# Attention with 512 heads on one core: other forms of loading K and V (4 KB rows, strided V, one head in eight transposed by DMA), and V fetched at K's lead

## Chip, cores, metric

The kernel runs on one core of a Trainium2 chip. The metric is the device time of one execution in microseconds (us); quoted times are medians of several executions. All executions told of here were fast (granted TensorE clock 0.96 to 1.00). One core has a matrix engine (TensorE, "PE" in the profile, its weight loads "PEld"), a vector engine (VectorE, "DVE"), an activation engine (ScalarE, "ACT"), GpSimd ("POOL"), and SyncE ("SP"), which in this kernel does nothing but issue DMAs.

## The reference

```python
B, H, Sq, Sk, D = 16, 32, 192, 1024, 128          # bf16
def reference(q, k, v):
    scale = q.shape[-1] ** -0.5
    scores = jnp.einsum("bhqd,bhkd->bhqk", q, k) * scale
    return jnp.einsum("bhqk,bhkd->bhqd", softmax(scores, axis=-1), v)
```

There are 512 heads, worked on as 256 pairs. Each head has 256 KB of K, 256 KB of V, 48 KB of Q and 48 KB of output.

## The kernel before

The products need K with D on the partitions, so TensorE transposes each head's K: a batch of 16 transposes goes into one PSUM bank (`f_k`) and VectorE copies it to `f_kt`. Then come the scores (`f_s`), the exponential on ScalarE (`f_pt`), P·V into a single output bank (`f_o`), and the normalisation on VectorE. GpSimd copies V from its landing ring (`f_vs`) to `f_vp`. Q is transposed by the DMA itself. K and Q have rings of four pairs, V a ring of ten.

```python
def load_k(p):                                     # 512 KB, rows of 2 KB
    if p >= R: e.wait_ge(s_tr, 2 * (p - R) + 2)    # R = 4: the ring's old K is transposed
    e.dma_start(kn[:, p % R, :]..., kf[2*p:2*p+2].rearrange("x (m t) d -> m x (t d)", t=T))
def load_q(p):                                     # 96 KB, transposed by the DMA
    if p >= R: e.wait_ge(s_qk, 2 * (p - R) + 2)    # the scores of the ring's old pair are done
    e.dma_start_transpose(qt[:, p % R], qf[2*p:2*p+2]...)
def load_v(p):                                     # 512 KB, ring of NVS = 10 pairs
    if p >= NVS: e.wait_ge(s_pv, p - NVS + 1)
    e.dma_start(vs[:, p % NVS], vf[2*p:2*p+2]...)
# ... SyncE's order in the steady part:
for n in range(NPR + 2):
    load_k(n + R); load_q(n + R)
    load_v(n - 2 + NVS)
    if (n - 2) % GP == 0: store((n - 2) // GP - 1) # GP = 4 pairs a store
# ... TensorE's order:
def step(n):
    for x in range(2):                             # x: the two heads of a pair
        qk(2 * n + x)                              # waits for Q, and for the old exponential
        tr(n + 1 + x, 1 - x)                       # one batch of K transposes; waits for K
        pv(n - 2, 12 * x, 12 * x + 12)             # half of P·V of the pair before last;
                                                   # the first half waits for the output bank
# ... VectorE, once a pair:
def onorm(p):
    dve.wait_ge(s_pv, p + 1)
    dve.reciprocal(ri, O[:, :, 128]); dve.tensor_tensor(ob..., O..., ri..., ALU.mult)  # then s_on
```

Of the kernel before, what the change touches and what calls it, by code (L numbers as in the profile page):

```python
# [395 lines left out]
HINT = False  # L396
# [6 lines left out]
def _attention_kernel(nc, q, k, v, out, NVS=10):  # L403
# [3 lines left out]
    NH = B * H  # L407
# [14 lines left out]

    with ExitStack() as outer:
# [6 lines left out]
        s_kn = [sem("f_kn%d" % i) for i in range(R)]  # L430
        s_q = [sem("f_q%d" % i) for i in range(R)]
        s_v = [sem("f_v%d" % i) for i in range(NVS)]
# [13 lines left out]
        with ExitStack() as es:  # L446
# [7 lines left out]
            kn = sb("f_kn", [128, R, 2 * T * D], BF16)  # L454
# [3 lines left out]

            vs = sb("f_vs", [128, NVS, 2, T * D], BF16)
# [11 lines left out]

            block = es.enter_context(nc.Block())

            @block.sync
            def _(e):
                def load_k(p):
                    if p >= R:
                        e.wait_ge(s_tr, 2 * (p - R) + 2)
                    e.dma_start(
                        kn[:, p % R, :].rearrange("m (x c) -> m x c", x=2),  # L480
                        kf[2 * p:2 * p + 2].rearrange("x (m t) d -> m x (t d)", t=T),
                    ).then_inc(s_kn[p % R], 16)

                def load_q(p):
                    if p >= R:
                        e.wait_ge(s_qk, 2 * (p - R) + 2)
                    e.dma_start_transpose(
                        qt[:, p % R, :, :],
                        qf[2 * p:2 * p + 2].rearrange("g (p j) d -> (g p) (j d)", j=3),
                    ).then_inc(s_q[p % R], 16)  # L490

                def load_v(p):
                    if p >= NVS:
                        e.wait_ge(s_pv, p - NVS + 1)
                    e.dma_start(
                        vs[:, p % NVS, :, :],
                        vf[2 * p:2 * p + 2].rearrange("x (m t) d -> m x (t d)", t=T),
                    ).then_inc(s_v[p % NVS], 16)

                def store(g):  # L500
                    so = g % NSO
                    h0 = 2 * GP * g
                    last = GP * (g + 1) == NPR
                    if last:
                        e.wait_ge(s_fin, 1)
                    else:
                        e.wait_ge(s_rc, GP * (g + 1) + 1)
                    e.dma_start(
                        of[h0:h0 + 2 * GP].rearrange("(a x) (p j) d -> (x p) a (j d)", x=2, j=3),
                        ob[:, so, :, :],  # L510
                    ).then_inc(s_st[so], 16)

                load_k(0)
                load_q(0)
                load_k(1)
                load_q(1)
                load_v(0)
                for p in range(2, R):
                    load_k(p)
                    load_q(p)  # L520
                    load_v(p - 1)
                for p in range(R - 1, min(NVS, NPR)):
                    load_v(p)
                for n in range(NPR + 2):
                    if n + R < NPR:
                        load_k(n + R)
                        load_q(n + R)
                    if n >= 2 and n - 2 + NVS < NPR:
                        load_v(n - 2 + NVS)
                    if n >= 3 and (n - 2) % GP == 0:  # L530
                        store((n - 2) // GP - 1)
                store(NPR // GP - 1)
                for so in range(min(NSO, NPR // GP)):
                    e.wait_ge(s_st[so], 16 * len(range(so, NPR // GP, NSO)))

            @block.gpsimd
            def _(gp):
                gp.memset(ones[:], 1.0).then_inc(s_set, 1)  # L538
                gp.wait_ge(s_set, 1)
                gp.affine_select(  # L540
                    ident[:], ones[:], [[1, 128]], ALU.is_equal, 0.0, base=0, channel_multiplier=-1
                ).then_inc(s_set, 1)
                gp.memset(vp[:, :, :, D:VB], 1.0).then_inc(s_set, 1)  # L543
                for p in range(NPR):
                    gp.wait_ge(s_v[p % NVS], 16 * (p // NVS + 1))
                    if p >= R:
                        gp.wait_ge(s_pv, p - R + 1)
                    gp.tensor_copy(  # L548
                        vp[:, p % R, :, 0:D].bitcast(U32),
                        vs[:, p % NVS, :, :].rearrange("p x (t d) -> p (x t) d", d=D).bitcast(U32),  # L550
                    ).then_inc(s_vp, 1)

            @block.tensor
            def _(pe):
# [4 lines left out]
                def tr(p, y):  # L559
                    if y == 0:  # L560
                        take(s_kn[p % R], 16)
                    if (p, y) != (0, 0):
                        take(s_ev, 1)
                    ins = None
                    for t in range(T):
                        for z in range(2):
                            c0 = (8 * y + t) * D + 64 * z
                            ins = pe.transpose(  # L568
                                k_ps[64 * z: 64 * z + 64, t * 128: t * 128 + 128],
                                kn[:, p % R, c0: c0 + 64], ident[:], tile_position=(0, 64 * z))  # L570
                    ins.then_inc(s_tr, 1)

                def qk(h):
                    p, x = divmod(h, 2)
                    if x == 0:
                        take(s_q[p % R], 16)
                        if p == NPR - 1:
                            take(s_ev, 1)
                    if h >= 2:
                        take(s_exp, 1)  # L580
                    S = s_ps[x]
                    ins = None
                    for t in range(T):
                        cut = {2: (0, 2, 3), 5: (0, 1, 3)}.get(t, (0, 3))
                        for j0, j1 in zip(cut[:-1], cut[1:]):
                            mv = qt[:, p % R, j0:j1, 64 * x: 64 * x + 64]
                            c0 = t * SQ + j0 * 64
                            for w in range(2):
                                ins = pe.matmul(  # L589
                                    S[64 * w: 64 * w + 64, c0: c0 + (j1 - j0) * 64],  # L590
                                    kt[:, p % R, 8 * x + t, 64 * w: 64 * w + 64], mv,
                                    start=True, stop=True, tile_position=(0, 64 * w))
# [4 lines left out]
                def pv(p, lo, hi):  # L597
                    if lo == 0:
                        take(s_vp, 1)
                        if p >= NPR - 1:  # L600
                            take(s_exp, 2)
                        if p >= 1:
                            take(s_on, 1)
                    ins = None
                    for j, t in order[lo:hi]:
                        for x in range(2):
                            ins = pe.matmul(  # L607
                                o_ps[64 * x: 64 * x + 64, j * 129: j * 129 + 129],
# [7 lines left out]
                def step(n):  # L616
                    for x in range(2):
                        if n < NPR:
                            qk(2 * n + x)
                        if n + 1 + x < NPR:  # L620
                            tr(n + 1 + x, 1 - x)
                        if n >= 2:
                            pv(n - 2, 12 * x, 12 * x + 12)

                pe.wait_ge(s_set, 3)
                tr(0, 0)
                tr(0, 1)
                tr(1, 0)
# [3 lines left out]
                with nc.Fori(0, loops, engines=[mybir.EngineType.PE], hint_back_edge=HINT,  # L632
# [10 lines left out]
            def _(dve):  # L643
                cnt = [0]

                def done(ins):
                    ins.then_inc(s_dv, 1)
                    cnt[0] += 1
                    dve.wait_ge(s_dv, cnt[0])

                def evac(p, y):
                    dve.wait_ge(s_tr, 2 * p + y + 1)
                    if p >= R:
                        dve.wait_ge(s_qk, 2 * (p - R) + 2)
                    dve.tensor_copy(  # L655
# [3 lines left out]

                def onorm(p):  # L660
                    g, a = divmod(p, GP)
                    so = g % NSO
                    O = o_ps[:, 0:387].rearrange("p (j c) -> p j c", j=3)
# [4 lines left out]
                    if a == 0 and g >= NSO:  # L668
                        dve.wait_ge(s_st[so], 16 * (g // NSO))
# [7 lines left out]
                def check(lo, hi, i):  # L677
                    done(dve.tensor_scalar(chk[:, lo:hi], rinv[:, lo:hi], 1.0 / RS_HI, 1.0 / RS_LO, ALU.max, ALU.min))  # L678
                    done(dve.tensor_tensor(chk[:, lo:hi], chk[:, lo:hi], rinv[:, lo:hi], ALU.not_equal))  # L679
                    done(dve.tensor_reduce(bad[:, i: i + 1], chk[:, lo:hi], mybir.AxisListType.X, ALU.max))  # L680

                early = max(NPR - 6, 1)
                evac(0, 0)
                evac(0, 1)
                evac(1, 0)
                for n in range(NPR + 2):
                    for x in range(2):
                        if n + 1 + x < NPR:
                            evac(n + 1 + x, 1 - x)
                    if n >= 2:  # L690
                        onorm(n - 2)
                        if n - 2 == early - 1:
                            check(0, 3 * early, 0)
                check(3 * early, 3 * NPR, 1)
# [52 lines left out]
```

## Time and profile before

| before | |
|---|---|
| time | 984.85 us (981.81 to 985.28, four runs) |
| period of eight heads in the steady part | 14.67 us |
| first exponential; exponential of head 32; last exponential | 10.9; 86.9; 967.1 us |
| SyncE in one period: issuing / waiting on semaphores | 10.0 / 4.6 us |

The period is the mean distance between exponentials eight heads apart, over heads 48 to 464 of the trace.

The next lines are from the profile page of before: the span, the busy times, two groups of instructions (line, engine, operation, output<-inputs, count | busy us, mean ns of one | idle before it and what ended that), and the DMA issues (count, size, median us from issue to landing).

```profile
span 982.0 us, 67627 instructions
PE 948.1 (97%) x30722; PEld 945.6 (96%) x30722; DVE 546.1 (56%) x1031; ACT 743.6 (76%) x513; POOL 267.7 (27%) x263
...
L655 DVE COPY f_kt<-f_k 128x1024 bf16<-128x1024 bf16 x512 | 354.0, 691 | 408.6 <-PE f_k L568 408.6
...
L568 PE MATMUL f_k<-f_ident,f_kn 128*64 128x128 bf16 x8192 | 331.3, 220 | 18.5 <-PEq L557 18.5
...
f_kn<-in_k_dram SPq DMA_DIRECT2D x256, 512.0 KB, 5.9
f_vs<-in_v_dram SPq DMA_DIRECT2D x256, 512.0 KB, 5.1
...
f_qt<-in_q_dram SPq DMA_TRANSPOSE x256, 4.9
```

One stretch of 50 us from the windows view of before follows (busy us of each engine, granted clock, DMA share, GB/s).

```profile
core 0: us, PE busy (x) PEld busy (x) DVE busy (x) ACT busy (x) POOL busy (x), PEclk, DMA share, GB/s
...
450.00:500.00 50.00, 50.00 (x1645) 50.00 (x1642) 28.39 (x55) 39.65 (x28) 14.00 (x14) 1.00 1.08 349
```

TensorE is busy without a gap and limits the steady part. Of its 18.5 us of idle before K transposes, 16.6 lie in the first 60 us and 1.9 near the end, at 954. The DMA share of 1.08 says that the packets' times fill all 16 DMA engines as well. The timeline of TensorE in before (start, duration, line, what) shows one head:

```profile
516.95 0.86 PE L589 MATMUL f_s<-f_qt,f_kt 128*64 128x192 bf16 x20
517.62 0.64 PE L568 MATMUL f_k<-f_ident,f_kn 128*64 128x128 bf16 x16
518.07 0.89 PE L607 MATMUL f_o<-f_vp,f_pt 128*64 128x129 bf16 x24
518.77 0.86 PE L589 MATMUL f_s<-f_qt,f_kt 128*64 128x192 bf16 x20
```

From start to start, scores take 0.67 us, the batch 0.45 and half of P·V 0.70.

### The profile page before, as it was taken

The numbers are of one execution on the slowest core, as the hardware profiler recorded it, in microseconds if no ns is written. First come the engines' busy times: TensorE is split into PE (matmuls) and PEld (weight loads), VectorE is DVE, ScalarE is ACT, GpSimd is POOL, SyncE is SP. The second block draws the span as 40 slices with busy tenths as digits, with TensorE's granted clock in tenths as the row PEclk, the third lists the DMA queues.
The fourth block names the chain that finished last, engine by engine and source line by source line (L and its number), as shares of the span: only waits on it lengthen the run. The fifth ranks groups of instructions, "written<-read, shape, count | busy, mean of one in ns | idle before, by whom it ended". The sixth has DMA issues, their size and how long they took to land. (4 is left out here: it accounts for less than half of the span.)

```text
span 982.0 us, 67627 instructions
## 1 busy us (share of the span) xinstructions
PE 948.1 (97%) x30722; PEld 945.6 (96%) x30722; DVE 546.1 (56%) x1031; ACT 743.6 (76%) x513; POOL 267.7 (27%) x263
## 2 busy tenths in 40 slices
PE   5699999999999999999999999999999999999995
PEld 4699999999999999999999999999999999999995
DVE  2355555555556555555555555655555555565562
ACT  4377777777777777777777777777777777777773
POOL 2122222222222222222222222222222222222220
PEclk9799999999999999999999999999999999999998
DMA  9999999999999999999999999999999999999971
GB/s 296 256 259 349 351 347 325 354 329 353 329 348 343 332 342 341 346 328 342 351 326 344 334 350 320 361 340 301 367 349 335 350 316 347 358 336 335 347 235 38
DMA packets 279602, 319.35 MB, mean 325 GB/s; under 512 B 115712, under 2 KB 148480, under 8 KB 279552
## 3 DMA queue, kind: packets, MB, share of 16 engines
q1 hardware_dynamic: 279552, 318.84, 102.5%
q14 instruction: 37, 0.30, 0.1%
q8 instruction: 13, 0.21, 0.1%
HBM read 268.44 MB, written 25.17 MB: 299 GB/s over the span
## 5 line engine op out<-in xcount | busy, mean ns | idle before, releaser
L706 ACT ACTIVATE f_pt<-f_s 128x1536 bf16<-128x1536 f32 x512 | 742.4, 1450 | 224.1 <-PE f_s L589 223.9
L655 DVE COPY f_kt<-f_k 128x1024 bf16<-128x1024 bf16 x512 | 354.0, 691 | 408.6 <-PE f_k L568 408.6
L607 PE MATMUL f_o<-f_vp,f_pt 128*64 128x129 bf16 x12288 | 458.7, 221 | 2.2 <-PEq L557 2.2
L548 POOL COPY f_vp<-f_vs 128x1024 uint32<-128x1024 uint32 x256 | 266.8, 1042 | 694.0 <-PE f_o L607 678.9
L589 PE MATMUL f_s<-f_qt,f_kt 128*64 128x192 bf16 (+2 forms) x10240 | 443.5, 231 | 4.2 <-issue 4.2
L607 PEld LDWEIGHTS f_o<-f_vp,f_pt 128*64 128x64 bf16 x12288 | 394.9, 110 | 2.7 <-issue 2.7
L589 PEld LDWEIGHTS f_s<-f_qt,f_kt 128*64 128x64 bf16 x10240 | 359.8, 111 | 4.5 <-issue 4.5
L568 PE MATMUL f_k<-f_ident,f_kn 128*64 128x128 bf16 x8192 | 331.3, 220 | 18.5 <-PEq L557 18.5
L568 PEld LDWEIGHTS f_k<-f_ident,f_kn 128*64 128x64 bf16 x8192 | 288.3, 111 | 20.0 <-issue 19.8
L670 DVE TENSOR_TENSOR f_ob<-f_o,f_rinv 128x384 bf16<-128x384 f32 x256 | 142.7, 557 | 8.9
L666 DVE RECIPROCAL f_rinv<-f_o 128x3 f32<-128x3 f32 x256 | 46.2, 181 | 10.6 <-PE f_o L607 8.0
L706 ACT ACT_TABLE_LOAD x1 | 1.3, 1283 | 0.8 <-PEq L732 0.8
L639 PEld LDWEIGHTS f_o<-f_bad,f_ones 128*1 128x1 bf16 x1 | 0.1, 79 | 1.6 <-DVEq L695 1.6
L639 PE MATMUL f_o<-f_bad,f_ones 128*1 128x1 bf16 x1 | 0.2, 164 | 1.4 <-DVEq L695 1.4
L679 DVE TENSOR_TENSOR f_chk<-f_chk,f_rinv 128x750 f32<-128x750 f32 (+1 forms) x2 | 1.1, 560 | 0.1
L680 DVE TENSOR_REDUCE f_bad<-f_chk 128x1 bf16<-128x750 f32 (+1 forms) x2 | 1.1, 555 | 0.1
L678 DVE TENSOR_SCALAR f_chk<-f_rinv 128x750 f32<-128x750 f32 (+1 forms) x2 | 1.0, 508 | 0.0
L697 DVE CAST redo<-f_o 1x1 int32<-1x1 f32 x1 | 0.1, 147 | 0.3 <-PE f_o L640 0.3
L540 POOL TENSOR_SCALAR_AFFINE_SELECT f_ident<-f_ones 128x128 bf16<-128x128 bf16 x1 | 0.3, 292 | 0.1
L538 POOL MEMSET f_ones<- 128x128 bf16 x1 | 0.2, 204 | 0.3 <-POOLq L732 0.3
L543 POOL MEMSET f_vp<- 128x128 bf16 x1 | 0.2, 211 | 0.0
L732 POOL MEMSET const-float32-0.0<- 128x1 f32 x1 | 0.1, 98 | 0.3 <-issue 0.3
(5 smaller groups left out, 0.5 us busy)
## 6 DMA issues: line engine op xcount, KB each, us to landing
f_kn<-in_k_dram SPq DMA_DIRECT2D x256, 512.0 KB, 5.9
f_vs<-in_v_dram SPq DMA_DIRECT2D x256, 512.0 KB, 5.1
out_dram<-f_ob SPq DMA_DIRECT2D x64, 384.0 KB, 5.0
f_qt<-in_q_dram SPq DMA_TRANSPOSE x256, 4.9
```

The costliest lines, as they stand in the source:

```text
L548: gp.tensor_copy(vp[:, p % R, :, 0:D].bitcast(U32), vs[:, p % NVS, :, :].rearrange("p x (t d) -> p (x t) d", d=D).bitcast(U32),).then_inc( ...
L568: ins = pe.transpose(k_ps[64 * z: 64 * z + 64, t * 128: t * 128 + 128], kn[:, p % R, c0: c0 + 64], ident[:], tile_position=(0, 64 * z))
L589: ins = pe.matmul(S[64 * w: 64 * w + 64, c0: c0 + (j1 - j0) * 64], kt[:, p % R, 8 * x + t, 64 * w: 64 * w + 64], mv, start=True, stop=True ...
L607: ins = pe.matmul(o_ps[64 * x: 64 * x + 64, j * 129: j * 129 + 129], pt[:, (2 * p + x) % NP, t * SQ + j * 64: t * SQ + j * 64 + 64], vp[:, ...
L639: pe.matmul(o_ps[0:1, 0:1], ones[:, 0:1], bad[:, 0:1], start=True, stop=False)
L655: dve.tensor_copy(kt[:, p % R, 8 * y: 8 * y + 8, :], k_ps[:].rearrange("d (t c) -> d t c", c=128),).then_inc(s_ev, 1)
L666: dve.reciprocal(ri, O[:, :, 128]).then_inc(s_rc, 1)
L670: dve.tensor_tensor(ob[:, so, a, :].rearrange("p (j d) -> p j d", j=3), O[:, :, 0:128], ri.unsqueeze(2).to_broadcast([128, 3, D]), ALU.mul ...
L678: done(dve.tensor_scalar(chk[:, lo:hi], rinv[:, lo:hi], 1.0 / RS_HI, 1.0 / RS_LO, ALU.max, ALU.min))
L679: done(dve.tensor_tensor(chk[:, lo:hi], chk[:, lo:hi], rinv[:, lo:hi], ALU.not_equal))
L680: done(dve.tensor_reduce(bad[:, i: i + 1], chk[:, lo:hi], mybir.AxisListType.X, ALU.max))
L706: act.activation(pt[:, h % NP, :], s_ps[h % 2][:], ACT_FN.Exp, scale=scale).then_inc(s_exp, 1)
```

## The change

The intent is to relieve TensorE: in each unit of eight heads (four pairs) the last head's K is transposed by the DMA, straight into `f_kt`, so TensorE does 448 batches and not 512. Below, "Kx" is the DMA that transposes this K, and a "period" is the time of one unit. To pay for Kx on the DMA's side, the K of the first three pairs comes in rows of 4 KB (for this K fewer, larger packets). That puts the keys in another order, so V of these six heads must land at every fourth partition: four strided DMAs of 384 KB, issued as one block of 1.5 MB. V is fetched only one unit ahead, at the lead of K, in place of ten pairs ahead. In each unit the slot after head 4 has no batch. There are smaller edits at the ends: eight dummy matmuls at the start, output banks that alternate in the last two pairs, a last store of one pair, and a check on VectorE spread over three steps.

```diff
-def _attention_kernel(nc, q, k, v, out, NVS=10):
+def _attention_kernel(nc, q, k, v, out, NVU=2):
                 def load_k(p):
+                    if p % R == 3:
+                        plain_k(p, 0, s_kn[3])                       # head 6 of the unit, 2 KB rows
+                        if p >= R:
+                            e.wait_ge(s_qk, 2 * (p - R) + 2)
+                        e.dma_start_transpose(                       # head 7: "Kx" below
+                            kt[:, 3, T: 2 * T, :], kf[2 * p + 1].rearrange("(m t) d -> m (t d)", t=T),
+                        ).then_inc(s_kx, 16)
+                    # ...
+                        e.dma_start(kn[:, p % R, :, :],
+                            kf[2 * p:2 * p + 2].rearrange("x (m s) d -> (x m) (s d)", s=2 * T))   # 4 KB rows
+                def load_va(u):                                      # "V block" below
+                    for c in range(4):
+                        e.dma_start(
+                            vs[c:128:4, u % NVU, 0:6, :],
+                            vf[h:h + 6].rearrange(
+                                "x (m b a t) d -> a b m x (t d)", b=2, a=2, t=T)[c // 2, c % 2],
+                        ).then_inc(s_va[u % NVU], 16)
                 for n in range(NPR + 2):
                     if n + R < NPR:
                         load_k(n + R)
                         load_q(n + R)
-                    if n >= 2 and n - 2 + NVS < NPR:
-                        load_v(n - 2 + NVS)
+                    u = n // R + 1
+                    if u < NPR // R:
+                        if n % R == 0:
+                            load_va(u)
+                        if n % R == 1:
+                            load_vb(u)                               # V of the unit's last pair, plain
# ... transposes of the 4 KB rows write every second pair of bf16 in PSUM:
+                            kp = k_ps[:, 256 * t: 256 * t + 256].rearrange(
+                                "d (m a b) -> d m a b", a=2, b=2)[:, :, a, :]
# ... TensorE's step (VectorE's likewise):
-                        if n + 1 + x < NPR:
-                            tr(n + 1 + x, 1 - x)
+                        if h < NH and h % 8 != 4:
+                            tr(7 * (h // 8) + h % 8 + (3 if h % 8 < 4 else 2))
# ... (semaphores, buffers, start and end cut)
```

## The prediction

> **What bounds it now.** In the steady part TensorE does: in the windows table from 400 to 550 us it is busy 50.00 of every 50 us at clock 1.00. The timeline shows exponentials on ScalarE every 1.833 us, one per head, 1.45 us long, so ScalarE is not the limit. Per head TensorE spends about 0.67 us on scores, 0.46 on a K transpose batch, 0.70 on half of P·V. 512 heads are 939 us; the other 43 us of the 982 us span are the ends. Beginning: from its seventh head on ScalarE is 17.4 us further behind than at its first; TensorE idles 9.6 us from 19.8 and 4.2 us from 44.2, because K and Q of pairs 4 onward stand in the DMA queue behind ten pairs of V; afterwards it restarts at a low clock (0.79 and 0.88 in the windows to 60 us). End: a 1.9 us gap at 954 behind the check on VectorE, two 1.0 us gaps where P·V waits for the single output bank, 7 us of last store.
>
> DMA is close behind: 340 GB/s, share 1.05-1.08 in those windows. But Q and K land about 7 us before use (landing median 4.9 and 5.9 us), so it is not the limit yet.
>
> **What the change does.**
> 1. 64 of 512 transpose batches leave TensorE, with their VectorE copies: QK start to PV start is 1.11-1.16 us with a batch, 0.67 without. 64 x 0.46 = 29 us, all critical.
> 2. Beginning: only four pairs of V ahead, K of head 0 first, eight dummy matmuls for the clock: 11-14 of the 17 us back.
> 3. End: check spread, output banks alternate, last store is one pair: 3-5 us.
> 4. DMA work rises. Packets in the trace take 18 ns (256 B), 36 (768 B), 84 (2048 B), 9 (semaphore): about 9 ns fixed each. The Trainium skill (DMA: Bandwidth & Descriptors, "Why small descriptors are slow") states a fixed per-packet overhead; the trace agrees. My estimate for 4 KB is 158 ns. Per four pairs and engine: before 13.9 us of packets in a 14.67 us period; after, 4 KB rows save 0.2, the transposed head (1024 packets of 256 B for 128 of 2 KB) costs 0.5: 14.2 us. TensorE's new period is 14.67 - 0.46 = 14.21. DMA and TensorE become equal, and DMA takes back some: period 14.2-14.6.
>
> Strided PSUM writes: the skill (PSUM - Partial Sum Buffer, "Specifications") says non-contiguous patterns slow matmuls. Here pairs of bf16 stay together; no line of this trace shows such a write. I expect no slowing, and little from V's stride.
>
> **Sum.** 985 - 29 (transposes) - 12 (beginning) - 4 (end) + 8 (DMA) = 948 us. Range 932 to 968. Faster by over 2%: 0.85; within 2%: 0.09; slower: 0.06.
>
> **What would show it.** Right: 448 K copies on VectorE, transpose matmuls at about the old 220 ns; no TensorE gap over 3 us in the first 60 us; exponentials averaging 1.78-1.82 us apart; Q and K landing later than before. DMA as the limit would show as short TensorE waits for K or Q, repeating every four pairs.
>
> **What would make it wrong.** Transposes into strided PSUM slower (0.44 us per batch more would cost 170 us). The DMA transpose holding the queue: transfers nearly stop for 0.5-1.7 us around Q transposes in this trace; one more per four pairs could eat the gain. V at stride four colliding within DMA. Or DMA gaining more from 4 KB rows, giving under 940.

## More of the kernel before

SyncE in one period: issuing / waiting on semaphores 10.0 / 4.6 us. SyncE's times are sums over 40 periods of the trace's DMA issue records, with the 0.04 us between them counted as issuing.

SyncE's timeline in before shows the even order, one V behind each K and Q, with free time (501.83 to 503.17) in which it waits:

```profile
499.50 1.19 SPq L487 DMA_TRANSPOSE f_qt<-in_q_dram  x1
500.73 0.59 SPq L495 DMA_DIRECT2D f_vs<-in_v_dram  x1
501.36 0.47 SPq L479 DMA_DIRECT2D f_kn<-in_k_dram  x1
503.17 1.19 SPq L487 DMA_TRANSPOSE f_qt<-in_q_dram  x1
```

## The result, and the profile after

| | before | after |
|---|---|---|
| time, us | 984.85 | 1074.07 (1070.18 to 1075.53, four runs) |
| ratio to before | | 1.0907 (95%: 1.0869 to 1.0945) |
| period of eight heads, us | 14.67 | 16.17 |
| exponential of head 32, us | 86.9 | 82.7 |
| last exponential to the end, us | 14.95 | 15.1 |
| SyncE in one period: issuing / waiting, us | 10.0 / 4.6 | 15.8 / 0.5 |

A ratio here is the mean time of one kernel's fast runs over that of the other's of the same rounds, so it is not quite the ratio of the medians quoted. The change made the kernel 9% slower. The steady part explains it: from head 32 on, 60 periods times 1.50 us are 90 us more; the beginning gives about 4 us back.

The page of after:

```profile
span 1068.6 us, 65473 instructions
PE 942.6 (88%) x29706; PEld 913.8 (86%) x29706; DVE 502.0 (47%) x967; ACT 743.6 (70%) x513; POOL 267.3 (25%) x263
...
L750 DVE COPY f_kt<-f_k 128x1024 bf16<-128x1024 bf16 x448 | 309.9, 692 | 538.0 <-PE f_k L656 535.8
...
L656 PE MATMUL f_k<-f_ident,f_kn 128*64 128x128 bf16 x7168 | 286.9, 219 | 91.2 <-PEq L630 88.5
...
f_kn<-in_k_dram SPq DMA_DIRECT2D x189, 512.0 KB, 7.2
f_vs<-in_v_dram SPq DMA_DIRECT2D x252, 384.0 KB, 5.6
...
f_kt<-in_k_dram SPq DMA_TRANSPOSE x64, 7.1
```

The 64 batches are gone (448 copies), and a transpose takes as long as before, 219 ns against 220, although it now writes with a stride. (Matmul ends are modelled in this profile; the starts say the same: from a batch to the next P·V 0.45 us in both.) But TensorE has 12% of the span idle (3% before), of which 91 us stand before K transposes. A K of 512 KB lands 7.2 us after its issue, not 5.9, and Kx after 7.1; a strided part of V, at 5.6, is little later than the 5.1 of before, the plain V of the unit's last pair lands after 7.0. A stretch of the windows view of after says the same, 45.4 us busy of 50:

```profile
450.00:500.00 50.00, 45.44 (x1452) 44.30 (x1448) 24.62 (x49) 36.05 (x26) 12.49 (x12) 1.00 1.02 309
```

The waits view of after counts them (who waited for whom: us in total, times, longest):

```profile
PE f_k L656 <- PEq L630: 88.5, 69, 4.2
PEld f_o L699 <- issue: 30.3, 65, 0.5
PE f_o L699 <- PEq L630: 18.1, 63, 0.3
```

Both kinds come once per unit: 69 and 63 times for 64 units. In the distances of the exponentials, by place in the unit, seven of the eight are 1.82 to 1.86 us as before, the one across the slot without a batch included (1.85), and the one from a unit's head 7 to the next unit's head 0 is 3.30 in place of 1.82. So two things went wrong: the removed batch saved nothing, and a stall of 1.48 us came in.

The timeline of after shows both:

```profile
512.40 0.56 DVE L770 TENSOR_TENSOR f_ob<-f_o,f_rinv 128x384 bf16<-128x384 f32 x1
...
513.11 0.89 PE L699 MATMUL f_o<-f_vp,f_pt 128*64 128x129 bf16 x24 [0.29 <-PEq L630]
...
518.67 4.59 SPq L519 DMA_TRANSPOSE f_kt<-in_k_dram  x1
...
523.30 1.26 SPq L534 DMA_TRANSPOSE f_qt<-in_q_dram  x1
...
524.61 0.58 SPq L526 DMA_DIRECT2D f_kn<-in_k_dram  x1
...
525.23 1.18 SPq L534 DMA_TRANSPOSE f_qt<-in_q_dram  x1
...
526.46 2.59 SPq L551 DMA_DIRECT2D f_vs<-in_v_dram  x4
...
529.09 0.60 SPq L526 DMA_DIRECT2D f_kn<-in_k_dram  x1
...
534.04 0.86 PE L680 MATMUL f_s<-f_qt,f_kt 128*64 128x192 bf16 x20
...
536.84 0.64 PE L656 MATMUL f_k<-f_ident,f_kn 128*64 128x128 bf16 x16 [1.94 <-PEq L630]
```

*The slot without a batch (513).* It lies between scores of an even head and the first half of the next P·V, which needs the single output bank. The pair before has just been normalised, 512.40 to 512.96, and P·V starts at 513.11, after a wait. Before, the batch filled this time. The weight loads' 30.3 us of waits, 65 times, stand where the 29 us were to be saved; e1 below tests this.

*The stall (536.84).* SyncE starts Kx at 518.67, and the issue itself takes 4.59 us. Then come Q, K, Q, the V block, and only then, at 529.09, the K that TensorE wants next; the trace has it land at 536.55, 7.46 us later. TensorE finished the scores before it at 534.9 and waits 1.94 us. Between 517.82 and 529.69 SyncE has no gap of more than 0.05 us. Over the steady part it waits 0.5 of 16.2 us and is busy issuing for the rest. That is the row of the table that changed most, and the prediction has no term for it.

A warning on reading: the profile's list of SyncE's own waits puts 230.6 us, 63 times, to Kx waiting for scores. Releasers are inferred, and there the inference took an event that fell inside the long issue. The record's start is the better witness: in the median Kx starts 0.50 us after the issue before it, within 0.01 us of the exponential of the head whose scores it needs, and its issue then takes 3.9 us. So the wait is 0.5 us, and the rest is issue.

### The profile page after: what moved, and what is told of

Same layout as the page of the kernel before. It is cut to its first block, busy times and chain, and to the rows that moved or that the text cites. A ratio compares the mean times of both kernels' runs of the same rounds, so it can differ in the third digit from the quotient of the medians.

```text
span 1068.6 us, 65473 instructions
## 1 busy us (share of the span) xinstructions
PE 942.6 (88%) x29706; PEld 913.8 (86%) x29706; DVE 502.0 (47%) x967; ACT 743.6 (70%) x513; POOL 267.3 (25%) x263
## 5 line engine op out<-in xcount | busy, mean ns | idle before, releaser
L750 DVE COPY f_kt<-f_k 128x1024 bf16<-128x1024 bf16 x448 | 309.9, 692 | 538.0 <-PE f_k L656 535.8
L699 PEld LDWEIGHTS f_o<-f_vp,f_pt 128*64 128x64 bf16 x12192 | 392.1, 110 | 30.4 <-issue 30.3
L656 PE MATMUL f_k<-f_ident,f_kn 128*64 128x128 bf16 x7168 | 286.9, 219 | 91.2 <-PEq L630 88.5
L656 PEld LDWEIGHTS f_k<-f_ident,f_kn 128*64 128x64 bf16 x7168 | 246.1, 110 | 105.4 <-issue 105.3
L721 PE MATMUL f_o<-f_ones 128*128 128x512 bf16 x8 | 3.6, 630 | 1.1 <-POOL f_ones L605 1.1
```

The source lines that it names most:

```text
L656: ins = pe.transpose(kp[64 * z: 64 * z + 64], w[:, 64 * z: 64 * z + 64], ident[:], tile_position=(0, 64 * z))
L699: ins = pe.matmul(O[64 * x: 64 * x + 64, j * 129: j * 129 + 129], pt[:, (2 * p + x) % NP, t * SQ + j * 64: t * SQ + j * 64 + 64], vp[:, p ...
L721: pe.matmul(o_ps[:], ones[:], ones[:].unsqueeze(1).to_broadcast([128, 4, 128]), start=True, stop=True)
L750: dve.tensor_copy(kt[:, p % R, 8 * y: 8 * y + 8, :], k_ps[:].rearrange("d (t c) -> d t c", c=128),).then_inc(s_ev, 1)
```

## The experiments

The expectations name these theories. **O** (in e1): the slot waits for the output bank. **L** (late): the K behind Kx and the V block is issued too late, a matter of SyncE's order. **D**: the DMA engines cannot carry the load, the transpose of K (Kx) above all. **S** (shape): the form of V, its stride, slows the transfers. **X**: in d6 and d7, Kx costs much only together with strided V; in e8 and e11, the changed stream as such does not fit, 15.7 us per unit, whatever its order. "Slot" is the head whose batch is left out. All kernels e1 to e11 give correct results; d1 to d7 are wrong (they only move data, and the output is zeros). In what follows "before" is always the same rounds' 982 to 984 us.

### e1_skip_odd: the slot without a batch after head 5

```diff
-                        if h < NH and h % 8 != 4:
-                            tr(7 * (h // 8) + h % 8 + (3 if h % 8 < 4 else 2))
+                        if h < NH and h % 8 != 5:
+                            tr(7 * (h // 8) + h % 8 + (3 if h % 8 < 5 else 2))
```

> The changed kernel, but the slot without a K transpose batch is moved from the first head of a pair to the second head of a pair (fifth slot of eight to sixth). Theory O (in the old slot P.V waits about 0.3 us for the single output bank to be read, so the slot stays 1.85 us long and the removed batch saves nothing; in the new slot P.V continues an accumulation and waits for nothing): one of the eight exponential intervals drops from 1.85 to about 1.4 us. Theory L (the stall of 1.48 us per eight heads is a late K that hangs on an earlier event of TensorE by a fixed chain of issue and landing) and theory D (the DMA engines cannot carry the load) both say that the saved 0.45 us per eight heads returns as a longer stall before the K transpose, because what arrives late does not arrive earlier: total 1065 to 1080 us. If the stall keeps its 1.48 us, total about 1045 us.

Measured: 1078.36 us, ratio 1.0952. The distance from head 5 to 6 fell from 1.85 to 1.42 us, so the removed batch now saves 0.43 us. The total did not fall: the stall grew from 3.30 to 3.85, and the period is 16.35. TensorE's timeline of e1 at the slot shows scores, P·V, scores without a wait:

```profile
521.77 0.86 PE L680 MATMUL f_s<-f_qt,f_kt 128*64 128x192 bf16 x20
522.43 0.89 PE L699 MATMUL f_o<-f_vp,f_pt 128*64 128x129 bf16 x24
523.16 0.86 PE L680 MATMUL f_s<-f_qt,f_kt 128*64 128x192 bf16 x20
```

It follows that the chosen slot was the reason why nothing was saved (the second half of P·V needs no free bank), as O said, and that something other than TensorE's work sets the period.

### e2_v_later and e7_v_later_2k: the V block one pair later

In e2 the V block stands behind the K and Q that were late, and V of the last pair one pair later too. e7 adds 2 KB rows and one plain DMA for the block's six heads.

```diff
-                        if n % R == 0:
-                            load_va(u)
                         if n % R == 1:
+                            load_va(u)
+                        if n % R == 2:
                             load_vb(u)
```

> The changed kernel, with the V block of six heads issued one pair later, so that K and Q of pair 4u+1 stand ahead of its 1.5 MB in the queue; the last V pair moves one pair later too. Bytes, rows and packets are the same. Theory L (lead: K of pair 4u+1 is issued 7.1 us after the scores that free the buffer, behind the K transpose and the V block, and lands 7.4 us later, more than the 14.2 us there are): the stall of 1.48 us per eight heads falls to under 0.4 us, total 985 to 1005 us. Theory D (throughput): the wait only moves to another load, the period of eight heads stays near 16.2 us, total 1055 to 1080 us.

> The order of e2 (V block one pair later; 1027 us, 15.47 us per eight heads) with the rows of e4 (K in 2 KB rows, six heads of V in one plain DMA). Theory S, together with L: once the order is mended the slow V stream is what is left, so plain rows now help, to under 14.9 us per eight heads and under 995 us, although they did nothing in e4. If V's partitions do not matter in the kernel: 1015 to 1040 us like e2.

Measured: e2 1027.10 us (1.0447), period 15.47; e7 1016.61 us (1.0363). The stall at head 7 to 0 vanished (1.82) in e2 and half of it came back at head 1 to 2 (2.48 for 1.82), in front of the next K, which is now the one behind the block. L has the direction right and missed by some 20 to 40 us; e7's 15.2 us per unit is about as good, so plain rows still matter little. In e2 SyncE waits on semaphores 0.04 us per period, so it issues all the time. That alone does not make SyncE the limit (see d1 below); but 15.47 is also the pace of the changed stream with no computing (15.45 in the steady part of d2).

### e3_no_kx: no DMA transpose of K

The eighth head comes plain and TensorE transposes it; all other new forms stay, 512 batches.

```diff
-                        if p >= R:
-                            e.wait_ge(s_qk, 2 * (p - R) + 2)
-                        e.dma_start_transpose(kt[:, 3, T: 2 * T, :], ...).then_inc(s_kx, 16)
+                        plain_k(p, 1, s_kn[3])
```

> The changed kernel with the eighth head loaded plainly and transposed on TensorE like the others: no DMA transpose of K, 512 batches again; 4 KB rows, V at every fourth partition and V's order and lead stay. Theory D (it is the DMA transpose with its 256-byte packets and its stop of the queue that the engines cannot carry): back to the old period of 14.67 us, total 965 to 985 us (ends are better than before). Theory L: about 1.2 us of issue and about 1.5 us of transfer leave the chain ahead of K of pair 4u+1, which is more than the stall, so also a stall near 0 and the same total; this run does not tell L from D but says what the transpose costs. Theory S (V's stride or V's lead alone are the cause): stall stays above 1 us, total above 1040 us.

Measured: 1006.09 us (1.0228), period 15.11. It was to be 985 or less. In this order most of the loss goes with Kx, and 0.41 us of stall per unit (2.23 for 1.82) stays with the V block alone.

### e4_rows_2k: neither 4 KB rows nor strided V

```diff
             def mixed(p):
-                return p >= R and p % R < 3
+                return False
-                            kf[2 * p:2 * p + 2].rearrange("x (m s) d -> (x m) (s d)", s=2 * T),
+                            kf[2 * p:2 * p + 2].rearrange("x (m t) d -> m x (t d)", t=T),
-                    for c in range(4):
-                        e.dma_start(vs[c:128:4, u % NVU, 0:6, :], ...)
+                    plain_v(h, 6, s_va[u % NVU])
```

> The changed kernel with all K in 2 KB rows and the six heads of V in one plain DMA of 2 KB rows; the DMA transpose of the eighth head, the order and the lead stay. Theory S (writing every fourth partition makes the engines collide, so V lands late): faster, under 1040 us. Theory D with my packet estimate (4 KB rows save 0.2 us of 14.2 us of packets per engine): slower by about 0.2 us per eight heads, 1080 to 1095 us. Theory L: the issue of V takes 0.6 instead of 2.6 us, so K of pair 4u+1 is issued 2 us earlier, but its data still stand behind the same 1.5 MB; landing decides, so a small gain of at most 0.5 us per eight heads, 1040 to 1075 us.

Measured: 1071.53 us (1.0894), period 16.21, the same as the changed kernel. S falls as the main cause: with the shapes of before, and the order of after, nothing is won.

### e5_v_per_pair, e6_v_per_pair_plain and e9_v_two_later: V pair by pair again

e5 is e4 with V issued per pair, directly behind that pair's K and Q (ring of eight pairs), and slot 5. e6 is e5 without Kx. e9 is e5 with V two pairs later.

```diff
                     if n + R < NPR:
                         load_k(n + R)
                         load_q(n + R)
-                    u = n // R + 1
-                    if u < NPR // R:
-                        if n % R == 0:
-                            load_va(u)
-                        if n % R == 1:
-                            load_vb(u)
+                        load_v(n + R)          # e9: load_v(n + 2), below Q
```

> The changed kernel with the DMA transpose of the eighth head kept, all rows 2 KB, V fetched pair by pair right behind K and Q of the same pair (a ring of eight pairs, so V never waits for a buffer), and the slot without a batch moved to the sixth of eight. No large block stands ahead of any K now. Theory L (the loss is order and lead): no TensorE stall, period of eight heads near 14.25 us, total 935 to 955 us. Theory D (the DMA engines cannot carry the transpose): period stays above 15 us, total above 990 us, with K or Q landing late all over the eight heads. In between, 14.7 to 15 us, both count.

> The same without the DMA transpose of K: 512 batches on TensorE, all rows 2 KB, V pair by pair at K's lead. DMA's load is that of the kernel before. Both theories: period 14.67 us, no stall, total 960 to 970 us (985 less the 12 to 17 us of the beginning and 3 to 5 us of the end). If V's short lead in time by itself hurts, the period is longer than 14.8 us.

> e5 (962 us) with each V load two pairs later, so that at the beginning two pairs of V less stand ahead of K. The beginning should gain 1 to 4 us and the steady part stay at 14.4 us: 955 to 962 us. If V's lead in time is needed, the period grows and the total exceeds 965 us.

Measured: e5 961.82 us (0.9781; 95%: 0.9753 to 0.9810), period 14.39; e6 975.67 us (0.9922), period 14.67; e9 963.06 us (0.9787). From e4 to e5 lie 110 us, and the only differences are V's order and the slot, of which e1 showed that the slot alone gives nothing. So the order and grouping of V's loads is what the change broke. Kx, with its 64 batches fewer, is worth 14 us in this order (e6 less e5). A stall of 0.15 us per unit is left in e5, at head 4 to 5 (2.00), and e9 shows that V's place does not matter for it. In e5 the issue of Kx takes 1.6 us on average, in the changed kernel 4.0. The totals of all three lie above the expected ranges, by 6.8 us (e5), 5.7 (e6) and 1.1 (e9): the periods came as L said, but the ends gave back less than assumed, and in e9 V two pairs later gained nothing at the beginning (head 32 at 81.2 us, in e5 at 81.3).

### e10_k_ahead: K in front of the waits

e5, with the plain loads of K one pair earlier in SyncE's order, ahead of the waits for scores that Q and Kx have.

```diff
+                load_k(R)
                 for n in range(NPR + 2):
+                    if n + R + 1 < NPR:
+                        load_k(n + R + 1)
                     if n + R < NPR:
-                        load_k(n + R)
+                        load_kx(n + R)         # Kx alone, with its wait
                         load_q(n + R)
                         load_v(n + R)
```

> e5 (962 us, 14.39 us per eight heads, its last stall of 0.16 us at the first K after the DMA transpose) with each plain K load issued one pair earlier, ahead of the wait for the scores that the DMA transpose and Q need; it needs only its own buffer, which is free by then. Theory L: the last stall goes, 14.2 to 14.3 us, 948 to 958 us. If the 0.16 us is DMA's throughput, 14.4 us and 962 us stay.

Measured: 951.16 us (950.96 to 952.43), ratio 0.9681 (95%: 0.9664 to 0.9697), period 14.25. It beats both kernels. All distances are 1.82 to 1.85 us but the one at the slot, 1.42. Lines of its page and of its windows view:

```profile
span 950.9 us, 65536 instructions
PE 923.6 (97%) x29706; PEld 917.6 (96%) x29706; DVE 502.2 (53%) x967; ACT 741.6 (78%) x513; POOL 267.7 (28%) x263
...
f_kn<-in_k_dram SPq DMA_DIRECT2D x189, 512.0 KB, 6.0
```

```profile
450.00:500.00 50.00, 50.00 (x1639) 50.00 (x1635) 27.61 (x54) 40.42 (x29) 14.60 (x14) 1.00 1.09 343
```

TensorE is the limit again, at 50.00 of 50, and K lands after 6.0 us. SyncE's timeline of e10 has V after every Q, and Kx takes 2.05 us where it took 4.59:

```profile
520.23 2.05 SPq L528 DMA_TRANSPOSE f_kt<-in_k_dram  x1
522.33 1.26 SPq L535 DMA_TRANSPOSE f_qt<-in_q_dram  x1
523.63 0.58 SPq L542 DMA_DIRECT2D f_vs<-in_v_dram  x1
524.26 0.47 SPq L519 DMA_DIRECT2D f_kn<-in_k_dram  x1
```

The period holds 12.0 us of issue and 2.25 us of waits.

### e11_after_k_ahead: the same on the changed kernel

e1 (all DMAs of the change, V block included) with K ahead as in e10; the same lines of the diff.

> The changed kernel with all of its DMAs and its V block as they are, the slot without a batch moved to the sixth (as e1: 1078 us, 16.35 us), and only the plain K loads issued one pair earlier, ahead of the wait for the scores and ahead of the V block. Theory L (1.48 us of stall is K's lead in the queue): the stall falls to under 0.6 us, under 15.0 us per eight heads, under 1000 us. Theory X (the stream as such takes 15.7 us, as it did alone): 15.4 to 16.3 us, 1020 to 1075 us, with K no longer the only late load.

Measured: 1022.11 us (1.0401), period 15.34; under 1000 was expected of L, 1020 to 1075 of X. The stall left head 7 to 0 (1.82) and stands at 1 to 2 (2.86), before the next K, which is now behind the block: issued at 516.79, landed at 524.23. SyncE waits for 0.04 us per period. So K ahead is not enough: as X said, the kernel falls to the pace that this stream has alone (15.45, d2). SyncE issues without a pause there, which by itself does not say whether SyncE or the DMA sets this pace.

### e8_v_spread: the four strided DMAs spread over four pairs

The changed kernel with one of V's strided DMAs per pair, a third V buffer, and slot 5.

```diff
-                    for c in range(4):
-                        e.dma_start(vs[c:128:4, u % NVU, 0:6, :], ...)
+                    e.dma_start(vs[c:128:4, u % NVU, 0:6, :], ...)      # c = (n + 2) % 4
```

> The changed kernel with all of its DMAs (4 KB rows, V at every fourth partition in four DMAs, DMA transpose), only spread: one of V's four DMAs per pair, with a third V buffer so that none waits; and the slot without a batch is the sixth of eight. Theory L alone (order and lead are the loss): like e5, 14.2 to 14.6 us per eight heads, 945 to 970 us. Theory X (this stream does not fit: 15.7 us per four pairs alone): above 15.5 us and 1010 us, with stalls no longer at one place.

Measured: 1137.95 us (1.1575), the worst, where L expected 945 to 970 and X over 1010 with stalls no longer at one place. In the trace (span 1143.6 us) one distance, head 4 to 5, is 4.86 us, so the stall does stand at one place. Between Kx and the next K now stand Q and two V's (one strided, the plain one of the last pair), and that K needs 6.9 us to land; SyncE in turn waits 3.9 us per period. Spreading alone does not give K its lead back; that this arrangement put the latest K in a worse place is my reading of the order, which no further run tested. The miss stands: I had counted how much V was in the queue, not which K stood behind what.

### d1 to d7: the DMAs alone

These move the same data in the same order with no computing; each DMA waits only for the last one in its own buffer. Two executions each. Three flags are varied: Kx, 4 KB rows, and V as the block (four strided DMAs) instead of pair by pair.

```diff
-                KX, STRIDE, ROWS4 = False, False, False      # d1: the stream of before
+                KX, STRIDE, ROWS4 = True, True, True         # d2: of after
+                KX, STRIDE, ROWS4 = True, False, False       # d3: Kx alone
+                KX, STRIDE, ROWS4 = False, True, True        # d4: of after without Kx
+                KX, STRIDE, ROWS4 = False, False, True       # d5: 4 KB rows alone
+                KX, STRIDE, ROWS4 = True, True, False        # d7: d2 with 2 KB rows
# d6: d2, the block as one plain DMA of six heads (1.5 MB)
```

> DMA alone, wrong result on purpose (stores zeros): all loads and stores of the kernel before, in its steady order (K and V in 2 KB rows, Q by DMA transpose), issued as soon as the buffer's previous load has landed; no compute. Both theories: faster than 14.67 us per four pairs, 860 to 930 us in all.

> DMA alone, wrong result on purpose: the loads and stores of the changed kernel in its steady order (4 KB rows for six heads of K, V of six heads in four DMAs at every fourth partition, one head of K by DMA transpose). Theory D: about 16 us per four pairs, over 1000 us. Theory L: 14.0 to 14.6 us, 900 to 940 us. Between 14.7 and 15.5 us (940 to 1000): the transpose alone would already eat the gain, and lead makes up the rest.

> DMA alone, wrong result on purpose: the stream of the kernel before (878 us alone) plus only the DMA transpose of one head in eight; all rows 2 KB, V plain. Theory D (the transpose is what costs): most of the 126 us between 878 and 1004 us is here, over 960 us. Theory S (V at every fourth partition is what costs): packets alone count, 0.33 us per four pairs by my packet estimate, and 890 to 915 us.

> DMA alone, wrong result on purpose: the stream of the changed kernel without the DMA transpose of K (that head is loaded plainly): 4 KB rows and V at every fourth partition stay. Theory S: 960 to 990 us. Theory D: 870 to 900 us.

> DMA alone, wrong result on purpose: the stream of the kernel before with six heads of K in 4 KB rows and nothing else changed (V plain, pair by pair). By my packet estimate 0.2 us per four pairs less than 878 us: 862 to 880 us. If 4 KB rows rather than V's partitions were what slows the stream, over 920 us.

> DMA alone, wrong result on purpose: the changed stream (1004 us alone) in its own order with the DMA transpose and 4 KB rows of K, but the six heads of V in one plain DMA. Theory X (the transpose of K costs much only together with V written to every fourth partition): 885 to 920 us. If the transpose and the 4 KB rows are the pair, or the block order of V: still over 960 us.

> DMA alone, wrong result on purpose: the changed stream in its own order with the DMA transpose and V at every fourth partition, but K in 2 KB rows. Theory X: 990 to 1030 us. If 4 KB rows are needed for the loss: 900 to 930 us.

| DMAs alone | Kx | K rows | V | us |
|---|---|---|---|---|
| d1 | no | 2 KB | per pair | 878.36 |
| d5 | no | 4 KB | per pair | 865.35 |
| d4 | no | 4 KB | block, strided | 862.61 |
| d3 | yes | 2 KB | per pair | 907.08 |
| d6 | yes | 4 KB | block, plain | 975.4 |
| d2 | yes | 4 KB | block, strided | 1004.5 |
| d7 | yes | 2 KB | block, strided | 1012.1 |

The prediction's packet sums hold one by one: Kx alone costs 28.7/64 = 0.45 us per unit (0.5 predicted), 4 KB rows save 13.0/64 = 0.20 (0.2 predicted), and the strided block costs nothing without Kx (d4 against d5; d4 lies even below the 870 us that D expected). Their sum would give 878 - 13 + 29 = 894 us. The stream of after takes 1004.5. The extra 110 us, 1.7 us per unit, appear only where Kx and the block meet. d6 shows that the stride is not needed for it (975 is still 81 over 894); with the stride it is 29 us more. So S and D (Kx by itself) each fall as a single cause, and so does X as d6 had it (885 to 920 us expected without the stride).

What the two do to each other can be seen in how long a store takes to land. In the block order it is issued right behind a Q, in d2 with Kx just before that Q, in d4 without. In the issue list of d4:

```profile
out_dram<-f_ob SPq DMA_DIRECT2D x64, 384.0 KB, 7.0
```

In that of d2:

```profile
out_dram<-f_ob SPq DMA_DIRECT2D x64, 384.0 KB, 3.6
```

In d4 the store lands 7.0 us after its issue; in d2, 3.6 us, so that little can stand before it there (in d3, where a V comes between, 5.3). SyncE never waits on a semaphore in d1 to d7 (under 0.05 us per period): even with the stream of before its issues fill the period (13.4 us in d1, where before itself needs 10.0 for the same DMAs). So the time of an issue is no fixed cost; here it grew when the DMAs were issued without a pause. My reading: in the block order Kx, Q, K, Q are issued in a row, transposes take long to issue and carry few bytes (in the timeline of after above 7.7 us of issue, 518.67 to 526.41, for Kx, Q, K and Q with 256 + 96 + 512 + 96 KB), the queue drains, and then the block floods it, so that the next Kx must wait for room: in the trace of after Kx's issue begins with 7 DMAs under way and ends with 4, in e5 with 5 and 3. This fits these numbers, but no run varied the depth of the queue, so it is not shown, and d3 speaks against its last part: there Kx begins with 7 under way too and takes 3.0 us to issue, longer than in d2 (2.1), and yet the stream loses only 0.45 us per unit. The packet records (middle of each trace) add a sign: 2 KB packets take 84 to 86 ns in the median everywhere, but on average 112 ns in d2 and 107 in d6 against 90 to 91 in d1, d3 and d4. A minority of packets takes much longer; whether they wait or are slowed is open.

## Why the prediction was wrong

It said 948 us, and 6% for slower. Point by point:

1. **"64 x 0.46 = 29 us, all critical."** This step failed. The batch was removed from a slot where P·V then waits for the single output bank: 30.3 us of waits in place of 29 us of work. e1 shows that the next slot saves 0.43 us of its distance, and e10 that it then counts in full: 14.67 - 14.25 = 0.42 us per unit, 27 us.
2. **"DMA and TensorE become equal, and DMA takes back some: period 14.2-14.6."** This step failed most, 16.17 measured. The term that was wrong is DMA's 14.2 us per period. The single sums were right (d3, d5; a 4 KB packet takes 159 ns in the trace, 158 estimated; the stream of before 878.36/64 = 13.7 us, 13.9 estimated), but the new stream needs 1004.5/64 = 15.7 us with nothing computing (d2; 15.45 in its steady part), because Kx and the V block together cost more than their sum. So about 0.8 of the 1.50 us lost per period is this stream itself; e2 and e11, with K moved, end near its pace (15.47, 15.34). The other 0.7 is order. Two things were missing in the prediction. SyncE's issuing was never costed: 10.0 us per period before, 15.8 after (part of this may be effect and not cause, see d1). And the order was not followed: "Q and K land about 7 us before use" was read off the old order, with a V of 512 KB behind each Q. In the new one Kx and 1.5 MB of V stand before one K, and its lead is gone. e4 to e5 (110 us for V's order and the slot) and e10 show that order and grouping decide; e2 and e11 show the stall moving with the place of the block.
3. **The risk list.** It named "the DMA transpose holding the queue ... one more per four pairs could eat the gain", and says that the trace of before already had 0.5 to 1.7 us of it. To give that 6% was a mistake of weight. Transposes into strided PSUM and V's stride, named beside it, were no danger in the kernel: 219 ns against 220, and e4 against the changed kernel (in the DMAs alone the stride costs nothing without Kx, d4 against d5, and 29 us with it, d6 against d2).
4. **"Beginning: ... 11-14 of the 17 us back."** Mis-sized. In e10, which has it without stalls, head 32's exponential comes at 80.0 for 86.9 us; 1.7 of these 6.9 us are four saved batches, so 5.2 are the beginning's. TensorE still has one gap of 4.2 us in the first 60 us of after.
5. **"End: ... 3-5 us."** In sum nothing: from the last exponential to the end 14.95 us before, 15.1 after, 15.9 in e10. The traces divide it. Up to the landing of the last store it is 9.6 us before and 6.9 in after and e10, so the edits gave 2.8 us; what follows that landing (drains and semaphores of all engines) grew from 5.3 us to 8.3 and 9.0, and no run says why.
6. **TensorE's new period, 14.21.** Right once the order is: 14.25 in e10. The prediction's 948 is near e10's 951, with smaller ends and no loss to DMA: 984.9 - 27.1 - 5.2 + 1 = 953.6.

The books: from head 32 to the last exponential, 60 periods, after takes 90.7 us more than before; up to head 32 it takes 4.3 less and at the end 0.2 more. That is 86.6 us, the difference of the two profiled spans; the medians differ by 89.2. After less e10 is 64 x 1.92 = 123 us, as measured (1074.07 - 951.16 = 122.9): of the 1.92 us, 0.43 are the slot and 1.48 the stall.

Still open: why exactly Kx and the V block slow each other with nothing computing (d2, d6), for which I have the reading above and no test; whether SyncE's issuing or the DMA sets the pace of that stream; and whether 4 KB rows and strided V could be kept in a good order (e8's way was worse).

## What to carry to other kernels

When loads change their form or grouping, write down the issuing engine's program for one period, with the measured issue time of every entry, transposes above all, and find for each consumer what stands between its load and the event that lets it go; a sum of bytes or packets does not see this. Issue times change with what is under way (Kx 1.6 to 4.0 us here), so the program is best checked by running the DMAs alone, as d1 to d7 do. Work removed from a busy engine is saved only where the next instruction may start at once, so look at that instruction's other waits before choosing the slot. Loads that need no wait belong in front of those that do, and a large prefetch went best in pieces next to the loads of the same pair (e5, e10); pieces alone do not help (e8).

## What the Trainium skill lacked or had wrong

- The Trainium skill, "DMA: Bandwidth & Descriptors", section "Issuing engines are not separate DMA queues", says the time to initiate a DMA "is usually small relative to the DMA itself". For a K of 512 KB in before that holds (issue 0.5 us, landing 5.9), for Kx in after it does not (4.0 and 7.1). And small shares add up on one engine: SyncE's issuing takes 15.8 of a 16.2 us period in the changed kernel, with 1.2 us for a Q transpose of 96 KB, 2.6 for the V block, and for Kx 1.6 (e5) to 4.0 (after).
- That page gives no time for the issue of a DMA transpose and does not say that it varies: it took 4.0 us in after, with 7 DMAs under way, and 1.6 in e5, with 5 (what makes it vary is not shown; d2 has 2.1 with 7), and all later DMAs of that engine stood behind it. Its section "Rules for kernel authors" says to issue early and wait late ("Overlap DMA with compute"), which agrees with e10 (951.16 us against 961.82 in e5); it does not say that a load placed behind another's wait or long issue is not early.
- The same page, "Why small descriptors are slow", gives a fixed overhead per packet; the trace agrees (18 ns for 256 B, 84 for 2 KB, 159 for 4 KB). It does not help with the combination: 894 us by sum, 1004.5 in d2.
- The Trainium skill, "PSUM - Partial Sum Buffer", "Specifications", says of PSUM's 8-byte cachelines that any non-contiguous pattern slows matmuls significantly. Transposes that write every second pair of bf16 took 219 ns, contiguous ones 220, and a batch 0.45 us from its start to the next P·V in both. The measurement decides for this pattern, which leaves pairs of bf16 together; the page has no such exception.
